# k and two experts' second weights through the hardware DMA queue as f32, rounded on GpSimd, with more loads under way

## The chip, the cores and the metric

The kernel runs on one core of a Trainium2 chip. The metric is device time in microseconds, the median of several executions. The kernel before has 235.01 us as the median of 3 runs (234.01 to 236.34). The engines are named PE (TensorE), DVE (VectorE), ACT (ScalarE), POOL (GpSimd) and SP (SyncE); 16 DMA engines serve the queues of the core.

## The reference

Two parts follow each other. The first is attention on q, k, v of shape (8 batches, 8 heads, 576 positions, 64): heads 0 to 3 see the last 32 positions, heads 4 to 7 every fourth of the last 128. The second is a soft mixture of experts on the 4608 tokens of 512 features, with 8 experts of 4 slots each and 1024 hidden features.

```python
scores = scale * np.matmul(q, k.transpose(0, 1, 3, 2))
mask_plain = (rel >= 0) & (rel < 32)
mask_dil = (rel >= 0) & (rel < 128) & (rel % 4 == 0)
attn = softmax(np.where(masks, scores, -1e9))
x = np.matmul(attn, v).transpose(0, 2, 1, 3).reshape(4608, 512)

logits = x @ phi                         # 4608 x 32
d = softmax over tokens of logits
slot_input = (d.T @ x).reshape(8, 4, 512)
slot_out[e] = np.maximum(slot_input[e] @ w1[e], 0) @ w2[e]
c = softmax over slots of logits
out = c @ slot_out                       # 4608 x 512
```

q, k, v are 9.4 MB each in f32, w1 and w2 16.8 MB each; the output is 9.4 MB.

## The kernel before, in words

Every piece of work is an `Op` with an engine or a choice of engines, a cost in microseconds, the buffers that it reads and writes, and a priority. `Prog.schedule` (L161) plays the ops through a model of the engines and writes out an order for each engine; `Prog.emit` (L242) turns the dependences into semaphore waits. The order on each engine is therefore fixed before the kernel starts, and its waits are what the plan's dependences need.

Three constants of the plan matter here. PE's instructions are counted in blocks of 127 matmuls (`BLOCK`), each a matmul with its weight load; a new block may not start sooner than 3.2 us after the one before (`SUPPLY`). A DMA has a size `bytes`, and the plan lets all of them pass one after the other at 400 KB a microsecond (L228 to L230). Loads marked `paced` wait until an earlier load has landed: the newest one behind which loads of at least 3.0 us (`COVER`) have been asked for (L186 to L191). That wait is a real semaphore wait on Pool.

Attention is worked in 16 units (`NSU`): unit n is batch n // 2 and four heads, the plain ones for even n and the dilated ones for odd n. A unit loads its k, q and v as 128 rows of 1152 bf16 columns each into one of nine staging slots of the tile `stg_all` (L357). `load` (L469) asks for each tensor in two DMAs of 64 rows from Pool's queue, which casts f32 to bf16 on the way. At the start the slots of units 0, 1 and 2 are asked for; later, after `stage_T` of unit n has been laid down, the loads of unit n + 3 follow (L937).

`stage_T` (L627) transposes the three slots on PE (L635 for even units, L638 for odd), and ACT or DVE copies the results to the tile `aren`. `stage_V` (L651) transposes v once more (L667), `stage_S` makes the masked scores (L690 to L699), `stage_P` the softmax and its transposes (L715 to L733), `stage_O` the weighted sums (L748 to L760), `stage_X` the transposes of the result (L778). After every second unit `gating` (L792) makes logits and running sums.

The expert weights are cast by Pool's queue too, in `load_w` (L486), four DMAs for each expert and layer. The first weights have a tile of their own, `w1b`. Six experts' second weights have `w2b`; those of experts 6 and 7 go into `stg_all` once attention has read the slots there for the last time (L956 to L960), and the last expert's are asked for in four column pieces. They have the lowest priority among the loads and all are paced. SP's queue carries phi at the start and the output at the end.

After the last unit come a short reduction, the expert stage (L1025 first layer, L1044 transposes, L1058 second layer) and the output (L1099 matmul, L1107 and L1108 copies, then DMAs from SP).

Of the kernel before, what the change touches and what calls it, by code (L numbers as in the profile page):

```python
# [13 lines left out]
DM = H * D  # L14
# [88 lines left out]
class Op:  # L103
    __slots__ = ("opts", "fn", "raw", "war", "prio", "rounds", "eng", "start", "end",
                 "sem", "val", "clock", "hard", "mm", "bytes", "dsem", "nleft", "users", "idx", "waits", "paced",
                 "more")


class Prog:
# [3 lines left out]
    BLOCK = 127  # L113
    SUPPLY = 3.2
    COVER = 3.0
# [6 lines left out]
    def op(self, opts, fn, r=(), w=(), a=(), rounds=(), prio=None, dma=None, extra=(), hard=(), mm=1,  # L122
           paced=False):
        o = Op()
        o.paced = paced
# [24 lines left out]
        for rd in o.rounds:  # L150
            rd.ops.append(o)
            if len(rd.ops) > 1:
                raw.update(rd.ops[:-1])
        raw.discard(o)
        war.discard(o)
        o.raw, o.war = raw, war - raw
        o.eng = None
        self.ops.append(o)
        return o

    def schedule(self):  # L161
        free = dict(PE=0.0, DVE=0.0, ACT=0.0, POOL=0.0, SP=0.0)
        dma_free = 0.0
# [20 lines left out]
        while ready:  # L184
# [57 lines left out]
    def emit(self, nc, blk):  # L242
# [6 lines left out]
        for o in self.order:  # L249
# [84 lines left out]
def bass_dilated_sliding_attn__then__soft_moe_slots_kernel(  # L334
# [68 lines left out]
    sm_all = stg_all[:, 8192:9408].bitcast(F32)  # L403
# [21 lines left out]
    b_stg = [Buf() for _ in range(NSLOT)]  # L425
# [24 lines left out]
    s_stg = [[nc.alloc_semaphore(f"s_stg{i}_{j}") for j in range(NPQ)] for i in range(NSLOT)]  # L450
# [18 lines left out]
    def load(w, paced=True):  # L469
        n, t = w // 3, w % 3  # L470
        b, ty = su_bt(n)
        i = w % NSLOT
        hs = (k, q, v)[t][b, 4 * ty:4 * ty + 4]
        if ty == 0:
            dst = slots[i].rearrange("p (h c) -> p h c", h=2)
            ap = hs.rearrange("(p x) (i c) d -> (x i) p (c d)", p=2, c=9)
        else:
            dst, ap = slots[i], hs.rearrange("h (i c) d -> (h i) (c d)", c=18)
        m = 128 // NPQ
        for j in range(NPQ):  # L480
            sl = slice(m * j, m * j + m)
            P.op(POOL, lambda g, sl=sl: g.dma_start(dst[sl], ap[sl]),  # L482
                 dma=(m * LSEQ * 5, s_stg[i][j]), paced=paced,
                 **(dict(w=[b_stg[i]]) if j == 0 else dict(a=[b_stg[i]])))

    def load_w(kk, e):  # L486
# [5 lines left out]
        m = 128 // NPW  # L492
        for i in range(n_p):
# [4 lines left out]
            else:  # L498
                sl = (slice(m * i, m * i + m), slice(0, c))
                bw = b_w  # L500
            P.op(POOL, lambda g, sl=sl: g.dma_start(dst[sl], ap[sl]), paced=True,  # L501
                 dma=(4 * DM * FF // n_p, sem[i]),
                 **(dict(w=[bw]) if i == 0 or bw is b_w2l[1] else dict(a=[bw])))
# [4 lines left out]
    for w in range(3):  # L508
        load(w, False)
# [4 lines left out]
    for w in (3, 4):  # L514
        load(w, False)
# [14 lines left out]
    for w in range(5, NSLOT):  # L530
        load(w)
# [95 lines left out]
    def stage_T(n):  # L627
# [12 lines left out]
        for t in range(3):  # L640
            rd = Round(ring, 2)
            i = (3 * n + t) % NSLOT
# [289 lines left out]
    for n in range(NSU):  # L932
# [4 lines left out]
        for w in range(3 * n + NSLOT, min(3 * n + NSLOT + 3, 3 * NSU)):  # L937
            load(w)
# [32 lines left out]
    for nb in (b_sab, b_siT, b_rep, b_frow):  # L971
        for bb in stg_of(8192, 9408):
            nb.r += bb.all_ops()
# [189 lines left out]
```

## Time and profile before

| what | value |
|---|---|
| median of 3 runs | 235.01 us |
| the profiled execution's own time | 236.88 us |
| its span, first to last instruction | 235.2 us |
| mean granted TensorE clock | 0.853 of full speed |
| PE, DVE, ACT, POOL busy | 173.6, 154.1, 135.8, 89.1 us |
| DMA: software queue (Pool) | 14208 packets, 30.94 MB written |
| DMA: hardware queue (SP) | 3312 packets, 9.50 MB |
| first matmul | 5.65 us |
| first expert matmul (L1025) | 197.46 us |
| Pool's k, q and v issues (L482) | 32 each, 0.56 us mean |
| Pool's weight issues (L501) | 32 for w1, 32 for w2, about 0.5 us mean |

Bytes are counted as written, so a cast load of 144 KB has read 288 KB. The profile's "issue" is time in which an engine waited for nothing that the profile shows. The DMA share is the mean over the 16 engines. The profile puts a wait down to the one releaser that came last.

### The profile page before, as it was taken

To read this page: it belongs to the slowest core of one execution; us is meant where nothing else is said; L and a number is where in the kernel's file an instruction comes from. 1 tells how busy PE (TensorE), PEld (TensorE's weight loads), DVE (VectorE), ACT (ScalarE), POOL (GpSimd) and SP (SyncE) were. 2 spreads that over 40 slices of the span, in tenths; PEclk is the share of its full clock that TensorE was granted. 3 is DMA by queue.
4 is the path that set the end of the run, shared out by engine and by line. 5 is a ranking of instruction groups with operands and counts; after the bars stand their busy time and mean duration, and the time that the engine had idled before them with its cause. 6 is when DMAs were issued, how large, how long until landed. Compare 5 with 4: busy or idle time off the path is not lost.

```text
span 235.2 us, 9729 instructions
## 1 busy us (share of the span) xinstructions
PE 173.6 (74%) x4406; PEld 123.7 (53%) x4406; DVE 154.1 (66%) x307; ACT 135.8 (58%) x204; POOL 89.1 (38%) x187
## 2 busy tenths in 40 slices
PE   0676868877997669968968967897887477984830
PEld 0464656655675556846755745665665243442310
DVE  3376578894869586479787773585558745649760
ACT  2479666765659537686969662689275330053550
POOL 7686745444235333444254344334333331000000
PEclk9999999995579995699999795599659855999796
DMA  6999999898979897699988998999999999129997
GB/s 87 177 147 157 147 161 145 132 171 120 172 142 154 126 171 142 104 173 150 165 133 145 179 167 143 172 187 202 180 178 178 188 186 170 23 91 407 403 406 302
DMA packets 17561, 41.06 MB, mean 175 GB/s; under 512 B 3440, under 2 KB 9584, under 8 KB 15600
## 3 DMA queue, kind: packets, MB, share of 16 engines
q0 software_dynamic: 14208, 30.94, 79.7%
q1 hardware_dynamic: 3312, 9.50, 10.4%
q8 instruction: 34, 0.56, 0.9%
q14 instruction: 7, 0.06, 0.1%
HBM read 61.93 MB, written 9.44 MB: 303 GB/s over the span
## 4 chain that ended last, share of the span: by engine, by line
PE 51%; DVE 17%; ACT 15%; issue 8%; DMA 4%; POOL 1%; DVEq 0%; POOLq 0%
ACT aren L330 9%; PE ps L667 8%; PE ps L638 6%; PE ps L699 5%; PE ps L635 5%; DVE aren L331 4%; PE ps L690 4%; PE ps L748 4%; DVE xn L760 4%; PE ps L778 3%; PE ps L727 3%; DMA stg_all<-in_v_dram 2%; ACT xt L330 2%; DVE aren L1108 2%; PE ps L1025 2%
## 5 line engine op out<-in xcount | busy, mean ns | idle before, releaser
L330 ACT ACTIVATE aren<-ps 128x1152 bf16<-128x1152 bf16 (+2 forms) x57 | 66.3, 1174 | 45.4 <-PE ps L667 27.9
L715 DVE TENSOR_REDUCE nm<-ps 128x10 f32<-128x640 f32 (+1 forms) x32 | 24.1, 754 | 15.1 <-PE ps L699 14.9
L331 DVE COPY aren<-ps 128x1152 bf16<-128x1152 bf16 (+2 forms) x23 | 26.6, 1164 | 8.4 <-PE ps L635 5.0
L667 PE MATMUL ps<-ident,aren 128*128 128x128 bf16 (+1 forms) x304 | 24.7, 240 | 4.1 <-DVE xn L760 2.0
L635 PE MATMUL ps<-ident,stg_all 128*64 128x128 bf16 x432 | 18.5, 244 | 10.6 <-DMA stg_all<-in_k_dram 5.7
L482 POOL DMA_DIRECT2D stg_all<-in_k_dram x32 | 17.9, 561 | 22.3 <-PE ps L635 7.3
L638 PE MATMUL ps<-ident,stg_all 128*128 128x128 bf16 x216 | 19.5, 243 | 9.3 <-ACT aren L330 5.1
L501 POOL DMA_DIRECT2D w1b<-in_moe_w_dram x32 | 16.0, 501 | 24.2 <-DMA w1b<-in_moe_w_dram 9.1
L760 DVE TENSOR_TENSOR xn<-ps,rv 128x576 bf16<-128x576 f32 x32 | 24.2, 758 | 1.1
L717 DVE TENSOR_TENSOR ps<-ps,nm 128x640 f32<-128x640 f32 (+1 forms) x32 | 24.3, 764 | 0.8
L482 POOL DMA_DIRECT2D stg_all<-in_q_dram x32 | 17.7, 560 | 16.9 <-PE ps L638 5.4
L667 PEld LDWEIGHTS ps<-ident,aren 128*128 128x128 bf16 (+1 forms) x304 | 19.2, 109 | 6.4 <-DVE xn L760 2.6
L482 POOL DMA_DIRECT2D stg_all<-in_v_dram x32 | 17.7, 559 | 12.3 <-DMA stg_all<-in_v_dram 3.6
L635 PEld LDWEIGHTS ps<-ident,stg_all 128*64 128x64 bf16 x432 | 15.0, 124 | 13.4 <-POOL ident L510 5.6
L748 PE MATMUL ps<-aren,pp 64*32 64x65 bf16 x1152 | 14.9, 197 | 9.6 <-issue 4.2
L638 PEld LDWEIGHTS ps<-ident,stg_all 128*128 128x128 bf16 x216 | 14.7, 109 | 12.8 <-ACT aren L330 6.5
L501 POOL DMA_DIRECT2D w2b<-in_moe_w_dram x24 | 11.7, 490 | 22.9 <-DMA w2b<-in_moe_w_dram 18.8
L720 ACT ACTIVATE pp<-ps 128x640 bf16<-128x640 f32 (+1 forms) x32 | 19.9, 666 | 0.6 <-DVE ps L717 0.5
L330 ACT ACTIVATE xt<-ps 128x512 bf16<-128x512 bf16 (+1 forms) x21 | 12.6, 636 | 11.1 <-PE ps L778 11.1
L699 PEld LDWEIGHTS ps<-aren 64*32 64x32 bf16 x1152 | 12.0, 98 | 12.2 <-issue 12.2
L699 PE MATMUL ps<-aren 64*32 64x64 bf16 x1152 | 16.3, 199 | 2.3 <-issue 2.3
L748 PEld LDWEIGHTS ps<-aren,pp 64*32 64x32 bf16 x1152 | 11.6, 93 | 11.9 <-issue 4.5
(138 smaller groups left out, 291.0 us busy)
## 6 DMA issues: line engine op xcount, KB each, us to landing
out_dram<-aren SPq DMA_DIRECT2D x17, 512.0 KB, 4.8
w1b<-in_moe_w_dram POOLq DMA_DIRECT2D x32, 256.0 KB, 5.6
w2b<-in_moe_w_dram POOLq DMA_DIRECT2D x24, 256.0 KB, 5.5
stg_all<-in_k_dram POOLq DMA_DIRECT2D x32, 144.0 KB, 4.4
stg_all<-in_q_dram POOLq DMA_DIRECT2D x32, 144.0 KB, 4.4
stg_all<-in_v_dram POOLq DMA_DIRECT2D x32, 144.0 KB, 4.6
stg_all<-in_moe_w_dram POOLq DMA_DIRECT2D x8, 256.0 KB, 5.6
out_dram<-aren SPq DMA_DIRECT2D x2, 256.0 KB, 2.2
```

Source lines behind the costliest of these rows:

```text
L330: return eng.activation(dst, src, ACTF.Copy)
L331: return eng.tensor_copy(dst, src)
L482: P.op(POOL, lambda g, sl=sl: g.dma_start(dst[sl], ap[sl]), dma=(m * LSEQ * 5, s_stg[i][j]), paced=paced, **(dict(w=[b_stg[i]]) if j == 0 ...
L501: P.op(POOL, lambda g, sl=sl: g.dma_start(dst[sl], ap[sl]), paced=True, dma=(4 * DM * FF // n_p, sem[i]), **(dict(w=[bw]) if i == 0 or bw ...
L635: ins = pe_.transpose(rd.h[64 * p:64 * p + 64, oc], sl[:, 576 * p + 64 * c:576 * p + 64 * c + 64], ident[:])
L638: ins = pe_.transpose(rd.h[:, oc], sl[:, oc], ident[:])
L667: ins = pe_.transpose(rd.h[row:row + nk, 128 * i:128 * i + 128], seq[u][:, 2, sl], ident[:])
L699: ins = pe_.matmul(rd.f[32 * j:32 * j + 32, 64 * (tile - t0):64 * (tile - t0) + 64], qk(u, p_, k, j, 1, 32, 0), qk(u, p_, k, j, 0, 64, 1), ...
L715: P.op([dve(ne)], lambda vv, sv=sv, nv=nv: vv.tensor_reduce(nv, sv(), AXX, AluOp.max), rounds=[rd], w=[b_nm[u][i]])
L717: P.op([dve(ne)], lambda vv, sv=sv, nv=nv, nt=nt: vv.tensor_tensor(sv(), sv(), nv.unsqueeze(2).to_broadcast([128, nt, 64]), AluOp.subtract ...
L748: ins = pe_.matmul(rd.f[32 * oq:32 * oq + 32, 103 * pl:103 * pl + 65], pt[u][sl, tile // 2, 32 * j:32 * j + 32], VOV[u][sl, pv, j % 2 if u ...
L760: P.op([dve(576)], lambda vv, cols=cols, rvp=rvp, p=p: vv.tensor_tensor(xn[x][:, :, p, :], cols(0, 64), rvp.unsqueeze(2).to_broadcast([128 ...
```

## The change

The k tensors of all 16 units come as f32 through SP's queue (`load_f32`), each in two DMAs, of rows 0 to 120 and of rows 121 to 127 (`ROWS`), into one of two f32 slots; Pool then rounds them by `tensor_copy` into one of three bf16 slots for k (`cast_k`). q and v keep Pool's casting DMAs and share six slots. The second weights of experts 3 and 4 (`W2_F32`) come the same way, in four column pieces each with a rounding for each; a piece is asked for when one of the first-weight loads has landed (`gate`). `w2b` holds five experts instead of six, and experts 5, 6 and 7 go to `stg_all`, which has 13 slots instead of 9. The first k loads after unit 0 wait for unit 0's v (`landed`). `load` now marks the DMAs that count for pacing.

In the plan `COVER` goes from 3.0 to 5.0. The one DMA clock becomes two: `some`, which all loads pass, and `rest`, which only Pool's loads pass and which each PE block takes for 0.95 us (`FETCH`). A DMA on Pool now waits for earlier work of Pool on its buffer.

```diff
@@ -111,8 +111,9 @@
     SLACK = 0.12
     DVE_MORE = 1.0
     BLOCK = 127
+    FETCH = 0.95
     SUPPLY = 3.2
-    COVER = 3.0
+    COVER = 5.0
     def __init__(self):
         self.ops = []
@@ -223,12 +226,17 @@
                 n_mm += o.mm
                 if n_mm > self.BLOCK:
                     n_mm, blk_t = n_mm - self.BLOCK, st
+                    rest = max(rest, st) + self.FETCH
             if o.paced and clk is not None:
                 o.raw = o.raw | {clk}
             if o.bytes:
-                dma_free = max(dma_free, o.end + 1.3) + o.bytes / 400e3
-                o.end = dma_free + 0.4
+                some = max(some, o.end + 1.3) + o.bytes / 400e3
                 if e == "POOL":
+                    rest = max(rest, o.end + 1.3) + o.bytes / 400e3
+                    o.end = max(some, rest) + 0.4
+                else:
+                    o.end = some + 0.4
+                if o.load:
                     loads.append((o, o.bytes / 400e3))
             order.append(o)
             ready.remove(o)
@@ -255,7 +263,7 @@
                     continue
                 need.append(d)
             for d in o.war:
-                if d.dsem is None and d.eng == e:
+                if d.dsem is None and d.eng == e and (e != "POOL" or o.dsem is None):
                     continue
                 need.append(d)
             if e == "POOL" and o.dsem is None:
@@ -349,13 +357,23 @@
         return A(nc.sbuf_tensor(name, shape, dt))
-    NSLOT = 9
+    NSLOT, NKS, NFS = 6, 3, 2
     SLOT = 1152
+    ROWS = (121, 7)
+    K_F32 = (0, 1, 2, 3, 4, 5, 6, 7, 8, 9, 10, 11, 12, 13, 14, 15)
+    W2_F32 = (3, 4)
     w1b = sb("w1b", [128, E_EXP, 4, FF])
-    N_W2R = 6
+    N_W2R = 5
     w2b = sb("w2b", [128, N_W2R, 8, DM])
-    stg_all = sb("stg_all", [128, NSLOT * SLOT])
-    slots = [stg_all[:, SLOT * i:SLOT * (i + 1)] for i in range(NSLOT)]
+    N_STG = NSLOT + NKS + 2 * NFS
+    stg_all = sb("stg_all", [128, N_STG * SLOT])
+    slots = [stg_all[:, SLOT * i:SLOT * (i + 1)] for i in range(NSLOT + NKS)]
+    fslots = [stg_all[:, SLOT * i:SLOT * (i + 2)].bitcast(F32)
+              for i in range(NSLOT + NKS, N_STG, 2)]
     VW = 18 * 2 * 66
     aren = sb("aren", [128, 6 * SEQW + 2 * VW])
     seq = [aren[:, 3 * SEQW * i:3 * SEQW * (i + 1)].rearrange("p (t c) -> p t c", t=3)
@@ -466,30 +487,67 @@
-    def load(w, paced=True):
-        n, t = w // 3, w % 3
+    def slot(n, t):
+        return NSLOT + n % NKS if t == 0 else (2 * n + t - 1) % NSLOT
+    def views(dst, n, t):
         b, ty = su_bt(n)
-        i = w % NSLOT
         hs = (k, q, v)[t][b, 4 * ty:4 * ty + 4]
         if ty == 0:
-            dst = slots[i].rearrange("p (h c) -> p h c", h=2)
-            ap = hs.rearrange("(p x) (i c) d -> (x i) p (c d)", p=2, c=9)
-        else:
-            dst, ap = slots[i], hs.rearrange("h (i c) d -> (h i) (c d)", c=18)
+            return (dst.rearrange("p (h c) -> p h c", h=2),
+                    hs.rearrange("(p x) (i c) d -> (x i) p (c d)", p=2, c=9))
+        return dst, hs.rearrange("h (i c) d -> (h i) (c d)", c=18)
+    def load(n, t, paced=True):
+        i = slot(n, t)
+        dst, ap = views(slots[i], n, t)
         m = 128 // NPQ
         for j in range(NPQ):
             sl = slice(m * j, m * j + m)
             P.op(POOL, lambda g, sl=sl: g.dma_start(dst[sl], ap[sl]),
-                 dma=(m * LSEQ * 5, s_stg[i][j]), paced=paced,
+                 dma=(m * LSEQ * 5, s_stg[i][j]), paced=paced, load=True,
                  **(dict(w=[b_stg[i]]) if j == 0 else dict(a=[b_stg[i]])))
-    def load_w(kk, e):
+    def load_f32(view, cost, extra=()):
+        i = n_f32[0] % NFS
+        n_f32[0] += 1
+        dst, ap = view(fslots[i])
+        for j, m in enumerate(ROWS):
+            sl = slice(sum(ROWS[:j]), sum(ROWS[:j + 1]))
+            P.op([("SP", 0.6)], lambda sp, sl=sl: sp.dma_start(dst[sl], ap[sl]),
+                 dma=(m * cost, s_fst[i][j]), extra=extra,
+                 **(dict(w=[b_fst[i]]) if j == 0 else dict(a=[b_fst[i]])))
+        return lambda to, n, **kw: P.op(
+            [("POOL", 1.2)], lambda g: g.tensor_copy(to, fslots[i][:, 0:n]), r=[b_fst[i]], **kw)
+    casts = {}
+    def load_k(n, extra=(), paced=True):
+        if n in K_F32:
+            casts[n] = load_f32(lambda dst: views(dst, n, 0), LSEQ * 6, extra)
+        else:
+            load(n, 0, paced)
+    def cast_k(n):
+        if n in K_F32:
+            casts[n](slots[slot(n, 0)], SLOT, w=[b_stg[slot(n, 0)]])
+    def load_w(kk, e, gate=()):
         src, c, dst, b_w, sem = ((moe_w1, 4, w1b[:, e], b_w1[e], s_w1[e]) if kk == "1" else
                                  (moe_w2, 8, w2v[e], b_w2[e], s_w2[e]))
         ap = src[e].rearrange("(p c) f -> p c f", c=c)
         last_one = kk == "2" and e == E_EXP - 1
         n_p = 4 if last_one else NPW
         m = 128 // NPW
+        if kk == "2" and e in W2_F32:
+            for i in range(4):
+                sl = slice(2 * i, 2 * i + 2)
+                cast = load_f32(lambda to: (to[:, 0:2 * DM].rearrange("p (c f) -> p c f", c=2),
+                                            ap[:, sl]), 6000, [gate[i]])
+                cast(dst[:, sl].rearrange("p c f -> p (c f)"), 2 * DM,
+                     **(dict(w=[b_w]) if i == 0 else dict(a=[b_w])))
+            return
         for i in range(n_p):
             if last_one:
@@ -498,21 +556,26 @@
             else:
                 sl = (slice(m * i, m * i + m), slice(0, c))
                 bw = b_w
-            P.op(POOL, lambda g, sl=sl: g.dma_start(dst[sl], ap[sl]), paced=True,
-                 dma=(4 * DM * FF // n_p, sem[i]),
-                 **(dict(w=[bw]) if i == 0 or bw is b_w2l[1] else dict(a=[bw])))
+            w_ops.append(P.op(
+                POOL, lambda g, sl=sl: g.dma_start(dst[sl], ap[sl]), paced=True, load=True,
+                dma=(4 * DM * FF // n_p, sem[i]),
+                **(dict(w=[bw]) if i == 0 or bw is b_w2l[1] else dict(a=[bw]))))
     P.cur = -1000
     small(lambda vv: vv.memset(ident[:], 0.0), w=[b_ident])
-    for w in range(3):
-        load(w, False)
+    load_k(0, (), False)
+    for t in (1, 2):
+        load(0, t, False)
+    landed = [P.ops[-1]]
+    cast_k(0)
     pool(lambda g: g.affine_select(
         out=ident[:], in_=ident[:], compare_op=AluOp.not_equal, fill=1.0, base=0,
         pattern=[[-1, 128]], channel_multiplier=1), w=[b_ident], r=[b_ident])
-    for w in (3, 4):
-        load(w, False)
+    load_k(1, landed, False)
+    for t in (1, 2):
+        load(1, t, False)
     for i in range(2):
         small(lambda vv, i=i: vv.memset(seq[i][:, :, 0:PAD], 0.0), w=b_seq[i])
         o = small(lambda vv, i=i: vv.memset(seq[i][:, :, PAD + LSEQ:SEQW], 0.0), a=b_seq[i])
@@ -527,8 +590,9 @@
     for j in range(1, 4):
         small(lambda vv, j=j: vv.tensor_copy(mbase[32 * j:32 * j + 32, :], mbase[0:32, :]),
               w=[b_mb], r=[b_mb])
-    for w in range(5, NSLOT):
-        load(w)
+    load_k(2, landed)
+    for t in (1, 2):
+        load(2, t)
     for u in range(2):
         P.op([("DVE", 0.4)], lambda vv, u=u: vv.tensor_copy(
             mask[u][:], mbase[:].unsqueeze(1).to_broadcast([128, 8, 64])), w=[b_mask[u]], r=[b_mb])
@@ -934,8 +998,12 @@
         P.cur = 100 * n - 60
         stage_T(n)
         P.cur = 100 * n - 100
-        for w in range(3 * n + NSLOT, min(3 * n + NSLOT + 3, 3 * NSU)):
-            load(w)
+        if n + 1 < NSU:
+            cast_k(n + 1)
+        if n + 3 < NSU:
+            for t in (1, 2):
+                load(n + 3, t)
+            load_k(n + 3)
         P.cur = 100 * n - 30
         stage_V(n)
         P.cur = 100 * n
@@ -953,15 +1021,25 @@
                 P.cur = 100 * NSU + 260 + n
                 combine(n // 4)
     P.more = 0.0
-    stg_of = lambda c0, c1: [b_stg[i] for i in range(c0 // SLOT, min((c1 - 1) // SLOT + 1, NSLOT))]
-    for i, e in enumerate(range(N_W2R, E_EXP)):
-        for bw in [b_w2[e]] + ([b_w2l[1]] if e == E_EXP - 1 else []):
-            for bb in stg_of(4096 * i, 4096 * (i + 1)):
-                bw.r += bb.all_ops()
+    seg = [(SLOT * i, SLOT * (i + 1), bb) for i, bb in enumerate(b_stg)]
+    seg += [(SLOT * (NSLOT + NKS + 2 * i), SLOT * (NSLOT + NKS + 2 * i + 2), bb)
+            for i, bb in enumerate(b_fst)]
+    stg_of = lambda c0, c1: [bb for a0, a1, bb in seg if a0 < c1 and c0 < a1]
     P.cur = 100 * NSU + 100
-    for kk in "12":
-        for e in range(E_EXP):
-            load_w(kk, e)
+    w_ops = []
+    order = [("1", e) for e in range(E_EXP)] + [("2", e) for e in range(E_EXP) if e not in W2_F32]
+    for kk, e in order:
+        if kk == "2" and e == E_EXP - 1:
+            for i, e_ in enumerate(W2_F32):
+                g0 = 8 + 4 * 4 * i
+                load_w("2", e_, w_ops[g0:g0 + 4 * 4:4])
+        if kk == "2" and e >= N_W2R:
+            i = e - N_W2R
+            for bw in [b_w2[e]] + ([b_w2l[1]] if e == E_EXP - 1 else []):
+                for bb in stg_of(4096 * i, 4096 * (i + 1)):
+                    bw.r += bb.all_ops()
+        load_w(kk, e)
     P.cur = 100 * NSU + 200
```

Left out are declarations, `stage_T`'s use of `slot(n, t)`, and `sm_all`, which moves to columns 12288 to 13504.

More of the change, by code (lines that the diff above doesn't have):

```diff
@@ L105 @@
                  "sem", "val", "clock", "hard", "mm", "bytes", "dsem", "nleft", "users", "idx", "waits", "paced",
-                 "more")
+                 "more", "load")
 class Prog:
@@ L122, in op @@
     def op(self, opts, fn, r=(), w=(), a=(), rounds=(), prio=None, dma=None, extra=(), hard=(), mm=1,
-           paced=False):
+           paced=False, load=False):
         o = Op()
+        o.load = load
         o.paced = paced
@@ L162, in schedule @@
         free = dict(PE=0.0, DVE=0.0, ACT=0.0, POOL=0.0, SP=0.0)
-        dma_free = 0.0
+        some, rest = 0.0, 0.0
         n_mm, blk_t = 0, 0.0
@@ L401, in bass_dilated_sliding_attn__then__soft_moe_slots_kernel @@
     last = sb("last", [128, 1], F32)
-    sm_all = stg_all[:, 8192:9408].bitcast(F32)
+    sm_all = stg_all[:, 12288:13504].bitcast(F32)
     sab = sm_all[:, 0:256].bitcast(BF16)
@@ L422, in bass_dilated_sliding_attn__then__soft_moe_slots_kernel @@
     blk = A(nc.Block())
-    b_stg = [Buf() for _ in range(NSLOT)]
+    b_stg = [Buf() for _ in range(NSLOT + NKS)]
+    b_fst = [Buf() for _ in range(NFS)]
+    n_f32 = [0]
     b_seq = [[Buf() for _ in range(3)] for _ in range(2)]
@@ L449, in bass_dilated_sliding_attn__then__soft_moe_slots_kernel @@
     NPQ, NPW = 2, 4
-    s_stg = [[nc.alloc_semaphore(f"s_stg{i}_{j}") for j in range(NPQ)] for i in range(NSLOT)]
+    s_stg = [[nc.alloc_semaphore(f"s_stg{i}_{j}") for j in range(NPQ)] for i in range(NSLOT + NKS)]
+    s_fst = [[nc.alloc_semaphore(f"s_fst{i}_{j}") for j in range(len(ROWS))] for i in range(NFS)]
     s_w1 = [[nc.alloc_semaphore(f"s_w1_{e}_{j}") for j in range(NPW)] for e in range(E_EXP)]
@@ L641, in stage_T @@
             rd = Round(ring, 2)
-            i = (3 * n + t) % NSLOT
+            i = slot(n, t)
             o = P.op(pe(0.47), lambda pe_, rd=rd, i=i: trs(pe_, rd, slots[i]),
@@ L971, in bass_dilated_sliding_attn__then__soft_moe_slots_kernel @@
     for nb in (b_sab, b_siT, b_rep, b_frow):
-        for bb in stg_of(8192, 9408):
+        for bb in stg_of(12288, 13504):
             nb.r += bb.all_ops()
```

## The prediction

> **What bounds the kernel now.** I read the page's slices first (busy tenths, granted clock and DMA share of 40 slices of 5.9 us), then its queues and its chain.
>
> ```profile
> PE   0676868877997669968968967897887477984830
> PEclk9999999995579995699999795599659855999796
> DMA  6999999898979897699988998999999999129997
> ...
> q0 software_dynamic: 14208, 30.94, 79.7%
> q1 hardware_dynamic: 3312, 9.50, 10.4%
> q8 instruction: 34, 0.56, 0.9%
> ...
> PE 51%; DVE 17%; ACT 15%; issue 8%; DMA 4%; POOL 1%; DVEq 0%; POOLq 0%
> ```
>
> Up to slice 34 (about 200 us) the DMA engines are busy nine tenths of the time, yet data waits are 4% of the chain and "issue", PE standing with nothing to wait for, is 8%: 0.08 x 235.2 = 18.8 us. Queue 8 carries PE's instructions: 34 packets of 16 KB, and 0.9% of 16 x 235.2 us over 34 is 1.0 us of one engine each. In the packet records an instruction packet takes 0.95 us in the median beside loads and 0.93 us at 206.9 us, where no load runs, so loads don't stretch it. What they do is hold back its start. PE's stalls fall where a block of about 256 PE instructions ends, and end about 1.35 us after the next packet. If a packet is asked for one block ahead, 31 packets between 18 and 190 us start 0.9 to 9.2 us after they are asked for, 2.9 in the mean; the one at 206.9 waits for nothing.
>
> The chain in order of time shows such stalls, and the first wait for data:
>
> ```profile
> 4.32 5.77 DMA stg_all<-in_v_dram
> ...
> 86.33 1.61 issue
> ...
> 119.74 1.36 issue
> ...
> 140.03 2.63 issue
> ...
> 197.46 4.08 PE ps L1025 x45
> ```
>
> The waits say who stood before what, how long in total, how often, and the longest:
>
> ```profile
> PEld ps L699 <- issue: 12.2, 34, 1.5
> ...
> POOL stg_all L482 <- PE ps L638: 8.3, 5, 2.7
> ...
> POOL stg_all L482 <- PE ps L635: 7.3, 3, 3.0
> ```
>
> Pool waits for PE to empty staging slots, not PE for loads after the first unit: q, k and v come early. The stream of loads binds nowhere by itself. Its last issue is this one in Pool's timeline (start, length, what, wait ahead):
>
> ```profile
> 195.96 0.54 POOL L501 DMA_DIRECT2D stg_all<-in_moe_w_dram  x1 [0.78 <-DMA stg_all<-in_moe_w_dram]
> ```
>
> With 5.6 us to land (the row of that group) it is there at 201.6; the last step of the second layer starts at 205.74 on the chain, so the weights have some 4 us to spare. So four parts set the end: the first loads, the pace of attention with its instruction stalls, the expert stage (197.5 to 208.3) and the output.
>
> **The change part by part.**
>
> *Removed from Pool:* 32 k issues x 0.561 us (their group) = 17.9 us and 8 second-weight issues x 0.490 = 3.9; together 21.8 us. *Added to Pool:* 16 roundings of 1152 columns and 8 of 1024. No row has this operation; Pool's select rows are nearest: 0.187 us for 1 column, 0.286 for 128, a slope of 0.78 ns a column, so 0.187 + 1152 x 0.00078 = 1.09 us and 0.99 us. Bounds: the shortest Pool row, 0.10, and the 128-column row scaled up, 2.6 us. I take 1.09 and 0.99: 25.3 us. Net +3.5 us on an engine busy 89 of 235 us: nothing on the path, covered by its waits (the two above alone are 15.6 us). A rounding that waits for its k holds q, v and weight issues behind it; with k asked for two units ahead, near 20 us, it should not. Without that cover one late rounding costs up to its 1.1 us.
>
> *Added to SP:* 48 issues at 0.605 us (the median of the phi issues), 29 us on a queue that is idle until 208 us: nothing. A k load waits there for its f32 slot; only phi (before) and the outputs (much later) share the queue.
>
> *Start.* Pool's q and v issues move ahead by the two k issues, 2 x 0.66 = 1.32 us (1.31 to 2.62 in its timeline). v ends the first wait, at 10.1 us. Its landing takes 5 us, in which the f32 k now competes with it: the gain lies between 0 and 1.3, and I take 1.2, since q and v also lose two loads ahead of them in their own queue; the rounding, near 5 plus 1.1, comes before v. The k of unit 1 now waits for that v: 8.9 + 4.4 to land (the row of k) + 1.1 is 14.4 us, where PE took it at 13.2 before. PE has unit 0's work meanwhile; of these 1.2 us I count 0.5. Start: -0.7, bounds -1.3 and +1.2.
>
> *DMA work.* Software loads: 30.94 MB in 0.797 x 16 x 235.2 = 3000 engine-us, 10.3 KB an engine-us. Removed are 16 k (295 KB) and two experts (1.05 MB): 458 + 204 = 662 engine-us. Plain copies of the hardware queue: 9.50 MB in 391 engine-us, 24.3 KB an engine-us, so f32 k (590 KB) and second weights (4.19 MB in all) cost 389 + 173 = 562. The total hardly falls. What matters is where it falls. No row shows how 121 rows are dealt to the engines; I assume equal shares, and 121 is 11 times 11. On an engine that the f32 rows don't use, 662 / 16 = 41 of 188 us are then gone, 22%; on one of eleven that carry them 51 come and 41 go. Bounds: 35 for 41 if all sixteen share, 562 if one carries everything, which would end the kernel far above any time given here and is left out as a remote case. The Trainium skill, "DMA: Bandwidth & Descriptors", "Why a DMA increments its semaphore by 16 and not by 1", says that a copy runs on the largest number of engines up to 16 that divides its rows, on the hardware queue on the lowest-numbered ones; that would be 11 engines, and no run here shows it yet.
>
> *Instruction stalls.* If the engine that fetches is one of the free ones, 22% less stands before its packets. I take the stall down in proportion: 0.22 x 18.2 (18.8 less the 0.6 at launch) = -4.0. Bounds: 0, if it is not free, and -18.2, if every wait went.
>
> *More under way.* COVER 5 for 3 lets 6 of the small loads (0.92 us in the plan) stay behind instead of 4, and 4 of the large ones (1.31) instead of 3. In before the packets asked for with 3, 4 and 5 loads under way started 2.6, 3.0 and 3.2 us later in the mean: +0.3 us a load, +0.6 for two. Of 31 x 2.9 = 90 us of such waiting 18.2 reached the path, a fifth: 31 x 0.6 / 5 = +3.7. The queue can be this deep only until the first weights and three second weights are in, then it runs empty: I take +1.5. Bounds: 0 and 31 x 0.6 = +18.6.
>
> *Second weights.* Three experts instead of two now wait for attention's slots: 12 loads at 1.29 us (spacing of Pool's issues from 192.08 to 195.96) after PE's last read of the slots at 174.2 make 189.7, plus 5.6 = 195.3, before their 205.7 by 10 us. Nothing. If attention shortens by more than 10, this is late next. *Reordering:* the plan is worked out anew and moves instructions on all engines; 0, within 2 either way.
>
> Sum: 235.2 - 0.7 - 4.0 + 1.5 = 232.0 us of span. The profiled execution took 236.88 us, 1.68 beyond its span and 1.87 above the runs' median 235.01; less 3.2, that median becomes **231.8**.
>
> **The rivals.**
>
> A. *The stalls shrink faster than the load.* With a full queue landings follow each other by 0.72 us for a 64-row load (8 to 13 us in the trace) and 1.29 for a weight load: 96 x 0.72 + 64 x 1.29 = 152 us, with 34 x 0.95 = 32 of instructions 184 of the first 190 us. On a free engine 64 x 0.72 + 56 x 1.29 + 32 = 150 remain; packets then often find it empty and start at once, as at 206.9. For it: the wait goes from 2.9 to 0 between those states. Against: pacing keeps the queue full while weights remain. Half the stalls gone and the same start: 235.0 - 9.1 - 0.7 = 225.2.
>
> B. *Nothing moves but the start.* The Trainium skill, "DMA: Bandwidth & Descriptors", "Issuing engines are not separate DMA queues", says that copies from all queues interleave on the same 16 engines and another queue saves only issue time; that speaks against this change. As a mechanism here: 562 engine-us replace 662 on all engines, instruction packets wait as before, and only the start's 0.7 us is won: 234.3. For it: the near-equal totals. Against: it needs an even spread, and 121 is no multiple of 16.
>
> C. *Slower: the deeper queue stands before the instructions.* Place: queue 8's packet on its engine. About 20 of the 31 packets land within 0.3 us of the moment when PE runs the first instruction of their block, so the loop of ask, wait, fetch sets PE's pace there, and 0.6 us more each is paid in full: 20 x 0.6 = +12, less 0.7 and 4.0: 242.3. It decides from where the wait grows by 0.24 us a packet (4.7 / 20). For it: the mean rises with loads under way. Against: means over 7, 18 and 7 packets, whose waits scatter from 0.9 to 9.2, carry little.
>
> D. *Slower: the fetching engine lies under the f32 rows.* Then 51 - 41 = 10 us are added to an engine that has 184 of 190 us; shared over attention, with a start that gains nothing because the f32 k holds q and v: +4 to +10, say 240. It decides from where the engine's 6 idle us are used up. For it: nothing in the profile names the engine, and eleven of sixteen are more than half. Against: the weights have 4 us to spare, and after 150 us no k is left to compete, so even then the price can stay near nothing, as in B.
>
> **How the numbers follow.** The forecast has 0.36, its own range 229.8 to 232.6 (2 down for reordering, 0.8 up for it and the start before it counts as B). A has 0.17, B 0.17, C 0.20, D 0.10. A measurement here tells about 1% from no change, 2.3 us: faster 0.36 + 0.17 = 0.53; same 0.17; slower 0.30. The range takes A's and C's times with a good half microsecond beyond A: 224.5 to 242.5.
>
> **What would show it.** Start: PE's first transposes of v near 9 us instead of 10.1, unit 1's k near 14. Stalls: "issue" in the chain near 15 us instead of 18.8 (A: 9; B: 18; C: above 24), with queue 8's 34 packets still at 0.95 us. Pool: roundings of 1.1 us, L482 issues down to 64. DMA: software queue near 62%, hardware near 25%. Tail from the first expert matmul to the end unchanged at 37.7 us. Wrong would be: PE or Pool waiting on k or on its rounding in attention, the expert stage waiting on second weights, or "issue" growing.

## The result, and the profile after

The changed kernel takes 257.34 us (median of 6 runs, 254.35 to 259.0) where the kernel before takes 236.48 us on the same chip: a ratio of 1.085, with a 95% interval of 1.075 to 1.095. Some executions of each kernel come out a few per cent slower than the rest, so this ratio and every ratio below that has an interval is taken over the faster ones, while times are medians of all (the medians alone give 1.088 here). The changed kernel is slower, and outside the range given. The profiled execution took 256.38 us, its span 254.6.

The page of the changed kernel, its slices, queues and the chain's shares:

```profile
PE   0589767887869495988786875879838547985840
PEclk9999955879977978579995899795985755798695
DMA  6999989869898839489599969995598989609997
...
q0 software_dynamic: 10240, 24.12, 53.2%
q1 hardware_dynamic: 7840, 23.14, 30.9%
q8 instruction: 34, 0.56, 0.9%
...
PE 52%; DVE 13%; issue 13%; ACT 13%; DMA 3%; POOL 3%; POOLq 0%; DVEq 0%
```

Two things stand out. The DMA engines are less busy in attention than before (slices at 3, 4 and 5 tenths where all were at 6 or more), so over the mean of the engines the loads have not run out of room. And "issue" is 13.3% of the chain: 0.133 x 254.6 = 33.9 us, against 18.6 before (18.8 in the prediction's rounding). That is 15.3 us more, in a span that grew by 19.4. The chain in order of time (start, length, what) shows the stalls longer than any before, and the first expert matmul 18.5 us later than its 197.46:

```profile
30.64 3.11 issue
...
85.83 3.79 issue
...
132.84 2.97 issue
...
154.94 2.88 issue
...
187.57 3.67 issue
...
216.00 4.72 PE ps L1103 x48
```

The waits of the changed kernel (who before what: total, times, longest):

```profile
POOL stg_all L507 <- PE ps L702: 27.0, 7, 10.0
...
POOL stg_all L522 <- PE ps L699: 20.9, 4, 7.2
...
PEld ps L763 <- issue: 19.4, 35, 3.8
...
POOL w2b L522 <- DMA stg_all<-in_moe_w_dram: 15.1, 3, 9.9
```

L763 is the line that was L699 before: its waits for instructions went from 12.2 us to 19.4, as often (35 and 34 times), the longest from 1.5 to 3.8. Pool waits even longer than before for PE to empty the slots, and its roundings (L522) wait for PE as well, not for data, until the second weights. So PE, not the stream of loads, sets the pace, and it stands waiting for its own instructions.

That it is instructions can be read from the packet records of queue 8, put beside the chain. Between 20 and 190 us the chain has 8 pieces of "issue" longer than 0.7 us in the kernel before and 12 in the changed kernel. Every one of the 20 ends between 1.22 and 1.65 us after the end of an instruction packet.

### The profile page after: what moved, and what is told of

It is laid out like the page before. It is cut to its first block, busy times and chain, and to the rows that moved or that the text cites. A ratio compares the mean times of both kernels' runs of the same rounds, so it can differ in the third digit from the quotient of the medians.

```text
span 254.6 us, 9769 instructions
## 1 busy us (share of the span) xinstructions
PE 180.6 (71%) x4406; PEld 130.1 (51%) x4406; DVE 154.4 (61%) x310; ACT 135.7 (53%) x201; POOL 93.4 (37%) x171
## 3 DMA queue, kind: packets, MB, share of 16 engines
q1 hardware_dynamic: 7840, 23.14, 30.9%
## 4 chain that ended last, share of the span: by engine, by line
PE 52%; DVE 13%; issue 13%; ACT 13%; DMA 3%; POOL 3%; POOLq 0%; DVEq 0%
PE ps L731 8%; ACT aren L338 7%; PE ps L699 6%; PE ps L791 5%; PE ps L763 5%; PE ps L702 4%; PE ps L842 4%; DVE aren L339 3%; PE ps L754 3%; DMA out_dram<-aren 3%; PE ps L812 3%; DVE xn L824 3%; PE ps L1103 2%; POOL stg_all L507 2%; DVE nm L779 2%
## 5 line engine op out<-in xcount | busy, mean ns | idle before, releaser
L338 ACT ACTIVATE aren<-ps 128x1152 bf16<-128x1152 bf16 (+2 forms) x55 | 65.5, 1201 | 44.4 <-PE ps L731 25.4
L339 DVE COPY aren<-ps 128x1152 bf16<-128x1152 bf16 (+2 forms) x25 | 26.1, 1046 | 15.6 <-PE ps L699 6.1
L699 PE MATMUL ps<-ident,stg_all 128*64 128x128 bf16 x432 | 22.2, 272 | 9.9 <-DMA stg_all<-in_q_dram 8.5
L522 POOL CAST stg_all<-stg_all 128x1152 bf16<-128x1152 f32 x16 | 18.5, 1156 | 23.6 <-PE ps L699 20.9
L781 DVE TENSOR_TENSOR ps<-ps,nm 128x640 f32<-128x640 f32 (+1 forms) x32 | 24.4, 763 | 0.7
L699 PEld LDWEIGHTS ps<-ident,stg_all 128*64 128x64 bf16 x432 | 18.3, 143 | 12.4 <-issue 9.1
L763 PE MATMUL ps<-aren 64*32 64x64 bf16 x1152 | 16.7, 201 | 9.8 <-issue 9.8
L338 ACT ACTIVATE xt<-ps 128x512 bf16<-128x512 bf16 (+1 forms) x20 | 12.3, 641 | 20.9 <-PE ps L842 20.9
L731 PEld LDWEIGHTS ps<-ident,aren 128*128 128x128 bf16 (+1 forms) x304 | 19.8, 111 | 6.2 <-DVE xn L824 2.8
L338 ACT ACTIVATE pp<-ps 128x1152 bf16<-128x1152 bf16 x14 | 15.9, 1132 | 13.1 <-PE ps L791 13.1
L812 PE MATMUL ps<-aren,pp 64*32 64x65 bf16 x1152 | 15.7, 205 | 9.0 <-issue 4.5
L763 PEld LDWEIGHTS ps<-aren 64*32 64x32 bf16 x1152 | 12.2, 98 | 19.4 <-issue 19.4
L791 PE MATMUL ps<-ident,pp 128*128 128x128 bf16 x144 | 16.9, 268 | 2.2 <-ACT pp L784 2.1
L702 PEld LDWEIGHTS ps<-ident,stg_all 128*128 128x128 bf16 x216 | 16.1, 116 | 4.4 <-ACT aren L338 2.3
```

What stands on the lines that cost most here:

```text
L338: return eng.activation(dst, src, ACTF.Copy)
L339: return eng.tensor_copy(dst, src)
L699: ins = pe_.transpose(rd.h[64 * p:64 * p + 64, oc], sl[:, 576 * p + 64 * c:576 * p + 64 * c + 64], ident[:])
L702: ins = pe_.transpose(rd.h[:, oc], sl[:, oc], ident[:])
L731: ins = pe_.transpose(rd.h[row:row + nk, 128 * i:128 * i + 128], seq[u][:, 2, sl], ident[:])
L763: ins = pe_.matmul(rd.f[32 * j:32 * j + 32, 64 * (tile - t0):64 * (tile - t0) + 64], qk(u, p_, k, j, 1, 32, 0), qk(u, p_, k, j, 0, 64, 1), ...
```

## The experiments

Ratios are to the kernel before on the same chip, with 95% intervals where given; "pieces" are the chain's "issue" pieces longer than 0.7 us between 20 and 190 us, added up (before 12.3 us, changed kernel 28.0). The theory at the start was that the f32 rows and the deeper queue hold back PE's instruction packets; the rivals were Pool's roundings, and a matter of which DMA engines carry the f32 rows.

### The depth alone: e1, e2

e1_cover3, in the changed kernel:

```
-    COVER = 5.0
+    COVER = 3.0
```

> The changed kernel with COVER back at 3.0, everything else kept. Depth theory (more loads under way hold back PE's instruction packets, rival C of the prediction): most of the 20 us come back, 236 to 242 us, 'issue' in the chain under 22 us. Rows theory (the f32 rows load the engine that fetches instructions, rival D): nothing comes back, 250 us or more, 'issue' above 30 us. Pool theory (roundings in Pool's queue hold the loads behind them): 248 us or more, Pool still 10 us at a time before PE.

251.67 us, 1.067 [1.033, 1.101]; pieces 19.9 us. By the medians 5.7 us are given back, less than the interval can tell from none.

e2_before_cover5, in the kernel before:

```
-    COVER = 3.0
+    COVER = 5.0
```

> The kernel before with COVER 5.0 alone. Depth theory: 247 to 256 us, 'issue' above 28 us, as in the changed kernel. Rows and Pool theories: within 1% of before, 233 to 238 us, since no f32 row and no rounding is there.

243.3 us, 1.029 [1.001, 1.057]; pieces 17.1. By the medians depth by itself costs some 6 us on either kernel, about a third of the loss. Both intervals are about 3% wide to each side, so the size is rough.

### The f32 loads: e4, e5

e4_no_f32, in the changed kernel:

```
-    K_F32 = (0, 1, 2, 3, 4, 5, 6, 7, 8, 9, 10, 11, 12, 13, 14, 15)
-    W2_F32 = (3, 4)
+    K_F32 = ()
+    W2_F32 = ()
```

> The changed kernel with no f32 load at all: k and all second weights by Pool's casting queue again; slots, plan constants and COVER 5 as changed. Depth theory: as slow as the changed kernel or slower, 252 to 262 us. Rows and Pool theories: back near before, 234 to 240 us.

242.1 us, 1.028 [0.998, 1.058]; pieces 14.5. Without f32 loads the changed kernel takes about what the kernel before takes with the deeper queue (e2, 243.3), though here 32% of the chain is waiting for loads; the rest of the 257.3 comes in with the f32 loads. This kernel is held up in another place than e2, so the agreement of the two times proves little; e7 below is the cleaner test.

e5_k_only, in the changed kernel:

```
-    W2_F32 = (3, 4)
+    W2_F32 = ()
```

> The changed kernel with only k as f32; all second weights by Pool's casting queue. Traffic theory: the 16 k loads are 389 of the 562 engine-us, so seven tenths of the step between no f32 load (242 us) and all (257 us): 250 to 254 us. If the second weights' pieces with Pool's 10 us wait for them are the cause: 241 to 246 us.

261.46 us, 1.115 [1.102, 1.128]; pieces 35.5. k alone carries the loss and more; 250 to 254 was the forecast. One of its stalls is longer than any in the changed kernel:

```profile
145.64 8.64 issue
```

It ends 1.30 us after a packet that began 6.40 us into it. Why that packet came so late was not settled, nor why k alone is 4 us slower than k with the second weights.

### Bytes or roundings: e7, e8

e7_thin_loads keeps every DMA, wait and rounding and the whole order of the changed kernel, but after the first two f32 loads it brings only 64 columns of each row, so that most of k, and of the second weights of experts 3 and 4, is old data:

```
-            P.op([("SP", 0.6)], lambda sp, sl=sl: sp.dma_start(dst[sl], ap[sl]),
+            thin = n_f32[0] > NFS
+            cut = (lambda v: v[sl]) if not thin else (
+                lambda v, sl=sl: v[sl, :, 0:32] if len(v.shape) == 3 else v[sl, 0:64])
+            P.op([("SP", 0.6)], lambda sp, to=cut(dst), fr=cut(ap): sp.dma_start(to, fr),
```

> The changed kernel with the same DMAs, waits, roundings and plan, but after the first two f32 loads each f32 load brings only a strip of its rows (64 of 1152 or 1024 columns), so k and the second weights of experts 3 and 4 are mostly not loaded. Traffic theory (the f32 bytes in the hardware queue hold back PE's instruction packets): 'issue' in the chain falls from 34 us to 24 or less, and the time to that of the kernel without f32 loads or below, 230 to 244 us. Pool theory (roundings that wait in Pool's queue, and the order planned around them): nothing changes, 250 us or more.

236.32 us, 1.004 [0.997, 1.011]; pieces 12.6: the loss is gone. The page of this kernel, queues and chain:

```profile
q0 software_dynamic: 10240, 24.12, 59.8%
q1 hardware_dynamic: 8864, 11.41, 14.9%
...
PE 47%; ACT 19%; DVE 15%; issue 9%; DMA 3%; POOL 3%; POOLq 0%; DVEq 0%
```

Against the changed kernel only q1's 23.14 MB have become 11.41, and "issue" fell from 13% to 9%. Its waits:

```profile
PEld ps L766 <- issue: 10.3, 34, 0.9
```

This is L763 of the changed kernel: 19.4 us became 10.3, the longest wait 3.8 became 0.9. The chain's 8 long pieces here, too, each end 1.35 to 1.52 us after an instruction packet.

e8_thin_roundings keeps the bytes and makes the roundings short:

```
+        full = n_f32[0] <= NKS or cost == 6000
...
-            [("POOL", 1.2)], lambda g: g.tensor_copy(to, fslots[i][:, 0:n]), r=[b_fst[i]], **kw)
+            [("POOL", 1.2)], lambda g, n=(n if full else 16): g.tensor_copy(
+                to[:, 0:n], fslots[i][:, 0:n]), r=[b_fst[i]], **kw)
```

> The changed kernel with the same loads and plan, but after the first three k only 16 columns of a k are rounded instead of 1152, so the roundings of k cost about 0.2 us instead of 1.16; most of k is left out. Pool theory: 13 x 0.95 = 12 us of Pool work less, 240 to 248 us. Traffic theory: unchanged, 251 to 259 us, 'issue' above 30 us.

255.94 us, 1.079 [1.051, 1.108]; pieces 24.4. Thirteen roundings became short, the time hardly moved. Its Pool groups (busy, mean ns, then idle ahead):

```profile
L523 POOL CAST stg_all<-stg_all 128x1152 bf16<-128x1152 f32 x3 | 3.5, 1154 | 0.1
L523 POOL CAST stg_all<-stg_all 128x16 bf16<-128x16 f32 x13 | 2.7, 206 | 25.6 <-PE ps L701 22.8 <-PE ps L704 2.6 <-issue 0.2
```

13 x 0.95 = 12.4 us of Pool's work went, the medians differ by 1.4 us and the ratios by half a per cent, and Pool waits a little longer for PE. The interval leaves room for some us, but not for the loss. This kernel, like e7, works on mostly old k, and it is not fast: so old data is not what made e7 fast.

### Which engines carry the rows: e3, e9, f1 to f4

e3_rows128, in the changed kernel, deals the f32 rows to all engines alike:

```
-    ROWS = (121, 7)
+    ROWS = (128,)
```

> The changed kernel with each f32 load in one DMA of 128 rows instead of 121 + 7. Rows theory: the engine that fetches carries 8 rows of each load instead of 12 or none; if it was under the eleven it gets relief, about 250 us; if it was one of the five free ones, it gets worse, 260 us or more. Depth theory: little changes, 254 to 260 us.

252.72 us, 1.073 [1.045, 1.101]; pieces 26.1: somewhat faster than 121 + 7 by the medians.

e9_rows125 puts them on few:

```
-    ROWS = (121, 7)
+    ROWS = (125, 3)
```

> The changed kernel with f32 rows in 125 + 3 instead of 121 + 7, so that a load should take 5 engines and 3 instead of 11 and 7, each with more than twice the bytes. If the fetching engine is under the eleven but not under the five: 'issue' falls to 24 us or less and the time to 240 to 247 us. If it is under the five: 'issue' above 40 us, 262 us or more. If the hardware queue holds the instruction packets back wherever its rows go: about the same as before the edit, 250 to 260 us.

284.82 us, 1.213 [1.192, 1.234]. The run can't speak for the stalls, since the loads themselves became the bound. Its chain and its waits:

```profile
DMA 72%; PE 9%; POOL 8%; issue 3%; DVE 2%; ACT 2%; SPq 1%; POOLq 0%; DVEq 0%
```

```profile
POOL stg_all L522 <- DMA stg_all<-in_k_dram: 50.5, 10, 9.4
POOL w2b L522 <- DMA stg_all<-in_moe_w_dram: 48.4, 8, 8.1
```

Ten of sixteen roundings of k and all eight of second weights now wait for their rows. That the number of rows sets the number of engines is seen in the semaphore events: a load of 121 rows ends with 12 arrivals (one at its issue, then 11), one of 7 rows with 8, of 125 with 6, of 128 with 16. So the Trainium skill's rule that the prediction cited from "DMA: Bandwidth & Descriptors", "Why a DMA increments its semaphore by 16 and not by 1" (the largest divisor of the rows up to 16) holds in the traces of the changed kernel, e9 and e3: 11 and 7, 5, and 16 engines.

To keep the loads off the bound, four kernels bring only k of even units as f32 and no second weights (`K_F32 = (0, 2, 4, 6, 8, 10, 12, 14)`, `W2_F32 = ()`), with four values of ROWS.

f1_even_121, `ROWS = (121, 7)`:

> The changed kernel with f32 loads for the k of the even units alone (8 loads), odd units' k and all second weights by Pool's casting queue, rows 121 + 7. This is the first of four that differ only in the rows, so in the engines that carry the same bytes: 11 and 7 here. Engine theory (the engine that fetches PE's instructions is one of those that carry the f32 rows, and not one of the first five): about a third of the step from no f32 load to all, 246 to 252 us, and the slowest or second slowest of the four. Queue theory (f32 bytes hold the instruction packets back wherever they go): all four within 2 us.

248.94 us (1.052 by the medians); pieces 27.5.

f2_even_125, `ROWS = (125, 3)`:

> The same with rows 125 + 3, so 5 engines and 3. Engine theory: instruction stalls as without f32 loads, 236 to 242 us, clearly under 121 + 7. Queue theory: as 121 + 7.

254.61 us (1.076); pieces 20.5, but now 12% of the chain waits for k, 0.12 x 250.8 = 30 us.

f3_even_119, `ROWS = (119, 9)`:

> The same with rows 119 + 9, so 7 engines and 9. If the fetching engine is the sixth or seventh, it carries 18 rows of a load instead of 12: slower than 121 + 7, 250 us or more. If it is the eighth to eleventh, it carries one row or none: near 125 + 3. Queue theory: as 121 + 7.

252.56 us (1.068); pieces 19.7, and 7% of the chain is k.

f4_even_128, `ROWS = (128,)`:

> The same with one DMA of 128 rows on all 16 engines, 8 rows each. Engine theory: the fetching engine carries 8 rows instead of 11 or 12, so between 125 + 3 and 121 + 7. Queue theory: as 121 + 7.

248.47 us (1.050); pieces 22.8.

Neither forecast held: the four lie 6 us apart, and 125 + 3 is the slowest. Freeing engines bought no time: with five or seven under the rows k comes late, and all sixteen are as good as eleven. Fewer engines do have less stalls in their profiles (20 us against 27), but each figure is from one execution, f1's from the longest of its four, and a chain that waits for k has fewer stalls left to show, so whether the fetching engine is among the eleven stays open. By the medians half the k costs 5% (f1), all of them 10% (e5).

### Does it grow with the bytes, and do depth and bytes add: g1 to g4

g2_half_loads, as e7 but with half of each row:

```
-                lambda v, sl=sl: v[sl, :, 0:32] if len(v.shape) == 3 else v[sl, 0:64])
+                lambda v, sl=sl: v[sl, :, 0:288] if len(v.shape) == 3 else v[sl, 0:v.shape[-1] // 2])
```

> The changed kernel, f32 loads after the first two bring only half of each row (576 elements; the rest of a strip keeps what it held), same DMAs, waits and roundings. If the cost grows with the f32 bytes, about half of the 21 us between e7_thin_loads (236.3) and the changed kernel (257.3): 247 us, chain issue about 27 us. If it comes with the packets' number or with any f32 traffic at all, near 257. If it comes only once the hardware queue is busy for most of an instruction block's time, near 238.

240.43 us where the kernel before took 233.77 beside it: 1.039 [1.023, 1.055]; pieces 17.1. By the ratios 0.4%, 3.9% and 8.5% for few, half and all of the columns: the cost grows with them, whether in proportion these intervals don't tell. e7 and g2 shorten each packet, so they can't tell fewer bytes from shorter packets; f1, with half as many k loads of full length, costs about half of e5. Nor do the bytes alone set the cost: e5 has fewer of them than the changed kernel (18.94 MB in q1 against 23.14) and takes longer.

g3_rows128_cover3, the changed kernel with both edits:

```
-    ROWS = (121, 7)
+    ROWS = (128,)
...
-    COVER = 5.0
+    COVER = 3.0
```

> The changed kernel with ROWS = (128,) and COVER 3.0. e1 (COVER 3.0 alone) took 251.7 and e3 (128 rows alone) 252.7, of 257.3. If the two are separate costs they add: 247 us. If both only thin out the same queue in front of the instructions, the second is worth little beside the first: 250 to 252.

246.24 us, 1.053 by the medians; pieces 19.3. If the two gains add, the medians of e1 (1.064), e3 (1.069) and the changed kernel (1.088) would give 1.045; if the second were worth nothing, 1.064. It lies between, and whether they add is not shown.

g4_thin_cover3, e7 with COVER = 3.0:

> e7_thin_loads (f32 loads after the first two bring only 64 columns of each row) with COVER 3.0 as well: what is left is the removal of 22% of the software queue's bytes with the depth of before. If depth costs 3.4 us per 1.0 whatever else is under way, 236.3 - 6 = 230 us, which is also what the prediction's first term alone (-4.0, with -0.7 for the start) would give from 235. If depth costs only together with the bytes taken away, 236.

235.02 us, 1.005 by the medians (the kernel before took 233.77 beside it); pieces 12.5. Without the bytes the depth costs nothing that shows (e7: 1.004). And with 22% of the software queue's bytes gone at the depth of before, the kernel is no faster than before.

g1_before_cover2, in the kernel before:

```
-    COVER = 3.0
+    COVER = 2.0
```

> The kernel before with COVER 2.0 in place of 3.0: fewer loads under way, nothing else. If every step of depth costs what 3.0 to 5.0 cost (243.3 against 236.4, 3.4 us per 1.0), and loads still come in time, about 233 us and a chain 'issue' share near 6%. If the units' loads come late with a shallower queue, PE or the transposes wait on DMA in the chain and the time is above 237 us. If the depth costs nothing below the software queue's own limit, 236.

256.36 us, 1.103 [1.086, 1.119]. The forecast that less depth is better failed. The chain of this kernel:

```profile
DMA 46%; PE 26%; DVE 10%; ACT 7%; issue 6%; POOL 2%; DVEq 0%; POOLq 0%
```

Waiting for loads is 46% of the chain where it was 4%; "issue" is down to 6%. At 2.0 the loads are late, at 5.0 the instructions are: the 3.0 of before is the best of the three.

### The second weights alone: h1, h2

h1_w2_only, in the changed kernel:

```
-    K_F32 = (0, 1, 2, 3, 4, 5, 6, 7, 8, 9, 10, 11, 12, 13, 14, 15)
+    K_F32 = ()
```

> The changed kernel with K_F32 empty: only the second weights of experts 3 and 4 come as f32, every k by the software queue, COVER 5.0. They are 8 f32 loads of 0.5 MB against the 16 of k. If each f32 byte costs the same, 8/24 of the 15 us between e4 (242.1) and the changed kernel (257.3): 247 us. If the second weights take from the software queue more than they cost in the hardware queue, as k alone being 4 us slower than both suggests, 238 us.

252.09 us, 1.086 [1.076, 1.096]; pieces 11.1. h2_w2_only_cover3 is the same with COVER = 3.0:

> The same with COVER 3.0. If depth costs 6 us as on the kernel before and on the changed one, 6 us below h1. By the byte rule 241; by the other 232 to 234, which would be at or below the kernel before.

259.16 us, 1.116 [1.103, 1.128]; pieces 13.8. Both forecasts missed, for a reason that neither theory had. h2's waits of Pool:

```profile
POOL w1b L560 <- DMA stg_all<-in_v_dram: 13.5, 6, 4.9
POOL w1b L560 <- DMA w1b<-in_moe_w_dram: 12.5, 11, 2.2
POOL w2b L522 <- DMA stg_all<-in_moe_w_dram: 12.4, 4, 7.8
```

PE's stalls are those of before. Pool stands at the rounding of a second weight (third line) with weight loads queued behind it, and the stream ends late: DMA is 32% of h2's chain. In the changed kernel the same wait (15.1 us) is not on the path; what makes the difference was not tried apart.

## Why the prediction was wrong

**The step that failed** is "DMA work", with the step on the stalls that builds on it. The sum counted 562 engine-us of f32 copies against 662 removed, took the total as unchanged, and gave the f32 traffic no price on PE, by the assumption that the fetching engine is "one of the free ones". The runs price it: the same program with all but a strip of these bytes left out takes 236.3 us and with them 257.3 (e7), so +21 us where the sum had nothing. The growing "issue" was one of the prediction's own signs of being wrong. Rivals C and D had the direction. D, with +4 to +10 us, had less than half of the price; it named one engine under the f32 rows, and the runs don't show that it is one, since spreading the rows over all sixteen is no worse.

**The size of the traffic** was off too: q1 grew from 391 engine-us to 0.309 x 16 x 254.6 = 1259, so the f32 loads took 868, not 562 (13.63 MB at 15.7 KB an engine-us, not 24.3); q0 fell from 3000 to 2167, by 833, not 662. The totals nearly cancel, as predicted. Yet the totals say nothing on PE: in the changed kernel the engines are less busy, and PE waits more. The Trainium skill's "Issuing engines are not separate DMA queues" ("DMA: Bandwidth & Descriptors") says that another queue saves nothing but issue time; the traces agree in the sense that bytes moved to the hardware queue still stand in the way, and by 8.5% they go beyond rival B's "nothing moves", 234.3 us.

**Instruction stalls, -4.0:** wrong at the depth of before, where 22% less software traffic (g4) left pieces of 12.5 us against 12.3 and a ratio of 1.005. At COVER 5 it is worth 1.029 to 1.004, about 6 us (e2 to e7), though these two kernels differ in more than that and their intervals overlap. If it holds, depth costs only while the queue is full of bytes, and the two are one effect, which the sum counted as two.

**More under way, +1.5:** mis-sized. It costs 6.9 us on the kernel before (e2) and 5.7 on the changed one (e1), nearer the +3.7 of its own working than the value taken, and about half of rival C's +12.

**Start, -0.7:** wrong in place, with little effect on the end. Pool's timeline of the changed kernel (start, length, what, wait ahead):

```profile
8.74 0.60 POOL L507 DMA_DIRECT2D stg_all<-in_q_dram  x1 [1.37 <-DMA stg_all<-in_q_dram]
9.34 1.16 POOL L522 CAST stg_all<-stg_all 128x1152 bf16<-128x1152 f32 x1
```

The first rounding stands behind a q issue that was itself held until an earlier load had landed, so PE transposed k and v together at 10.55 us instead of k at 5.65 and v at 10.14. e7 starts just as late and still ends as before.

**Roundings: right.** 1.09 and 0.99 us were worked out; here is the page's group of 16:

```profile
L522 POOL CAST stg_all<-stg_all 128x1152 bf16<-128x1152 f32 x16 | 18.5, 1156 | 23.6 <-PE ps L699 20.9
```

1.156 us, and by e8 the roundings of k are no large part of the path. **SP, second weights, tail: right** in the changed kernel: no wait of PE for weights on the chain, and 254.6 - 216.0 = 38.6 us of tail against 37.7. The cover was thin, though: in h1 and h2 Pool's wait at the f32 second weights ends late. **Reordering, 0:** g4, whose plan is new as well, ends 0.5% from the kernel before.

**What stays open.** On the chain "issue" grew by 15.3 us and PE's own work by about 12, while the parts of DVE and ACT fell by about 10, so the split of the 19.4 us is not sharp. PE's busy time rose from 173.6 to 180.6 us at a granted clock of 0.811 against 0.853. The clock isn't the main cause: one execution of e8 took 252.0 us at 0.848, one of e3 249.7 at 0.854. How the f32 bytes hold the packets back is not settled, but where the time goes is. The packets' median length went only from 0.95 to 1.02 us, and a stall ends as soon after its packet as before (1.39 us in the median, then 1.41). The packets start later: in the median 1.05 us ahead of the stall in the kernel before, 0.14 in the changed kernel, 0.97 in e7. What makes them start late, the bytes, the length of the f32 packets or one engine that carries both, is not known.

No version tried that computes the whole output beats the kernel before.

## What to carry to other kernels

A stream that has room for itself can still cost the compute engine its instructions. Where the chain shows "issue" that ends just after instruction packets, an added transfer has a price there that DMA engine time saved elsewhere doesn't show; a kernel that keeps every DMA and thins its bytes, like e7, measures it. Here, moving bytes to another queue didn't take them out of the way of the instructions, and equal totals were no proof of no effect. The depth of the load queue had an optimum between late data (2.0) and late instructions (5.0); look at both waits, on both sides, before moving it.

## What the runs showed of the hardware

f32 loads on the hardware queue, 24 of them in 48 DMAs, cost the kernel 21 us (e7 against the changed kernel) although the DMA engines' busy share between 20 and 190 us fell. The windows of that stretch, for the kernel before, the changed one, e7 and e1 in this order (length; busy us and instructions of PE, PEld, DVE, ACT, Pool; granted clock, DMA share, GB/s):

```profile
20.00:190.00 170.00, 134.29 (x3811) 101.53 (x3812) 119.51 (x214) 111.86 (x167) 70.80 (x139) 0.85 0.95 158
```

```profile
20.00:190.00 170.00, 129.96 (x3618) 99.91 (x3616) 111.55 (x199) 109.72 (x156) 69.47 (x118) 0.84 0.85 171
```

```profile
20.00:190.00 170.00, 132.29 (x3930) 100.53 (x3927) 122.88 (x222) 115.20 (x170) 79.87 (x137) 0.90 0.79 136
```

```profile
20.00:190.00 170.00, 127.62 (x3748) 100.41 (x3771) 116.77 (x208) 109.50 (x159) 70.32 (x118) 0.86 0.90 179
```

From before to the changed kernel to e7 the DMA share falls, 0.95, 0.85 and 0.79, while PE did 3811, 3618 and 3930 matmuls in the same 170 us: the share is no measure of how much the loads disturb PE. The bytes a second are none either: e1 has more of them than the changed kernel, 179 GB/s against 171, and still does more matmuls, 3748 against 3618.
